# Forgetting attention with a gated convolution FFN: three half batches loaded plainly, decay rows by DMA, a rewritten order

## The chip, the core and the metric

The kernel runs on one core of a Trainium2 chip. The metric is device time in microseconds (us). The profile names the engines so: PE is TensorE (matmuls), PEld its weight loads, DVE is VectorE, ACT is ScalarE, POOL is GpSimd, and SP is SyncE, which here only issues DMAs. "ACTq" and "SPq" are rows of the queues of ACT and SP, in which DMAs are issued. L12 means line 12 of the kernel; as the change adds lines, the same code has other line numbers after it.

## The reference, cut to what matters

```python
scores = scale * np.matmul(q, k.transpose(0, 1, 3, 2))        # (8, 8, 576, 576), scale = 1/8
cum    = np.cumsum(np.log(np.clip(f, 0.0001, 1.0)), axis=-1)
decay  = cum[:, :, :, None] - cum[:, :, None, :]
scores = np.where(causal, -1000000000.0, scores + decay)
attn   = softmax(scores)
x      = np.matmul(attn, v)          # 8 batches, 8 heads, 576 tokens, 64 per head -> (8, 576, 512)
h      = np.maximum(x @ w_in, 0.0)   # (8, 576, 1024)
conv   = sum of three taps over the tokens, each channel with its own weights
out    = (h * sigmoid(conv)) @ w_out # (8, 576, 512)
```

## The kernel before, in words

The 8 batches with 8 heads each are taken as 16 **half batches** hb of four heads; two neighbouring heads make a pair p. For each half batch q and k lie with the head's 64 dimensions on the partitions and the 576 tokens along the row, in tiles named `qk` (four in a ring, so half batch 4 takes the tile of half batch 0). A score block is a product of 128 columns of k with up to 512 columns of q, over all 128 rows: q and k come as float32 whose 16 upper bits are used as bfloat16, so odd rows hold the data and even rows would hold the lower halves. The even rows are overwritten: in a few of them stand the **decay rows** (the cumulated log gates, in two bfloat16 parts, against rows of one and minus one), so that one product gives score and decay together; the others are zero.

How q and k come in differs by half batch:

- Half batches 0 and 1 (`NPL = 2`) are loaded plainly into tiles `hg` (`load_plain`, tasks `ld`), turned by nine PE transposes of 128x128 for each pair and side (`turn_qk`, L165, tasks `tp`), and written into `qk` by ACT (L171) or DVE (L173) in one operation of 128 rows which also replaces the even rows by constants (`turned_qk`, tasks `cl`).
- Half batches 2 to 15 come by a transposing DMA from SP (L179, tasks `q`), and for 2 to 7 DVE then replaces the even rows (`clamp`, L185).
- The decay rows: the gates f are loaded twice, on 128 rows; DVE clips them (L519, task `dca`), ACT takes the logarithm (L265, `dcl`), DVE sums them up (L269, `dcs`) and writes the tile `kc` (L272, L273, `dck`). Three DMAs on SP write `kc` into a tensor `image` in DRAM (L278, `ki`), and for each half batch from 1 on two small DMAs bring its rows back into `qk` (L201 and L202, task `rw`). Half batch 0 does not wait for that (`PAIRS = 2`): each of its score products is followed by two more products, with `sel_k` and `kc` (L314) and with `kc` and `sel_q` (L316), which add the decay.

Per half batch, the score tasks are `st` (the last 64 tokens of the four heads), `sd` (diagonal blocks of a pair) and `so` (the blocks off the diagonal, one task for each head). Half batches 0 to 7 get their causal mask by a product with `mask` ahead of the diagonal blocks (L319), the others by POOL. ACT takes the exponentials: `et` (L331), `ed` (L352), `eo` (L369). Then follow the product with v (`pv`, L388 and L393; v is loaded in five pieces by `v` and cast to 16 bits by `va` on POOL, ACT or DVE), the normalization on DVE (`n` L402, `m` L404), and the turning of x (`t` L413 on PE with `tx` L416 on DVE, or one DMA).

When both half batches of a batch b are turned, its FFN runs over eight column blocks ff: product (`f`, L428), relu on ACT (`r`, L438), two convolution steps on DVE (`c` L444, `d` L446), tanh or sigmoid on ACT (`a`, L449), gate on DVE (`g`, L456, L454). When the eight gates are done, the second product (`o`, L463 and L467) runs in five chunks, each copied out by ACT or DVE (`e`, L473, L478) and stored (`s`).

**What sets the order.** The program text is one long list, `ORDER`, of some 1,070 task names; `Plan.play` emits the tasks in that order, so that each engine's queue is the list cut to its own tasks, run strictly one after the other. A name behind `@` is the engine or queue chosen for the task. Buffers are given out in the order of the list too. PE's results go through only four PSUM tiles, `ps` 0 to 3: a task that wants one waits until the reader of an earlier task has emptied it. An engine that waits for one task holds all that stands behind it in its queue.

## Time and profile before

| | |
|---|---|
| device time, three runs | 250.19, 250.32 and 251.66 us; median 250.32 |
| the profiled execution | span 249.0 us from the first to the last instruction; the page gives it no device time of its own, so the median of the runs stands 1.3 us above its span |
| PE, DVE, ACT, POOL busy | 230.2, 210.3, 206.7, 54.3 us |
| TensorE clock that the throttle granted | 1.000 of full speed over the whole span |
| DMA | 49.70 MB, mean 200 GB/s |

The busy time of PE says only that a matmul was under way, and short matmuls overlap; so the length of a task on PE is read from start to start, not from the durations of its matmuls. Rows of the timeline merge instructions of one line that follow each other ("x36"). A number in brackets, or behind the bar, is the idle time just before, and the arrow names what ended it. Rows of stretches give each engine's busy time between two moments.

### The profile page before, as it was taken

The numbers are of one execution on the slowest core, as the hardware profiler recorded it, in microseconds if no ns is written. First come the engines' busy times: TensorE is split into PE (matmuls) and PEld (weight loads), VectorE is DVE, ScalarE is ACT, GpSimd is POOL, SyncE is SP. The second block draws the span as 40 slices with busy tenths as digits, with TensorE's granted clock in tenths as the row PEclk, the third lists the DMA queues.
The fourth block names the chain that finished last, engine by engine and source line by source line (L and its number), as shares of the span: only waits on it lengthen the run. The fifth ranks groups of instructions, "written<-read, shape, count | busy, mean of one in ns | idle before, by whom it ended". The sixth has DMA issues, their size and how long they took to land.

```text
span 249.0 us, 6606 instructions
## 1 busy us (share of the span) xinstructions
PE 230.2 (92%) x2723; PEld 148.7 (60%) x2723; DVE 210.3 (84%) x326; ACT 206.7 (83%) x280; POOL 54.3 (22%) x76
## 2 busy tenths in 40 slices
PE   0898989769999999999999999999999999999992
PEld 0786675447755675666566756576675557454440
DVE  5727077999999999989999979999989899999840
ACT  2754985999998999998998899998999997678632
POOL 8001500051300040045005352229240420000000
PEclk9999999999999999999999999999999999999999
DMA  7979999999999999999999999899999930705055
GB/s 188 303 165 235 270 211 209 220 175 279 256 186 222 196 176 276 239 234 197 196 305 240 227 204 200 203 232 202 216 178 303 176 106 22 163 0 192 0 191 190
DMA packets 120849, 49.70 MB, mean 200 GB/s; under 512 B 109919, under 2 KB 111455, under 8 KB 120819
## 3 DMA queue, kind: packets, MB, share of 16 engines
q1 hardware_dynamic: 120573, 48.91, 92.0%
q8 instruction: 21, 0.34, 0.6%
q10 hardware_dynamic: 246, 0.37, 0.6%
q14 instruction: 9, 0.07, 0.1%
HBM read 21.11 MB, written 10.17 MB: 126 GB/s over the span
## 4 chain that ended last, share of the span: by engine, by line
PE 69%; DVE 9%; ACT 8%; DMA 6%; SPq 4%; issue 2%; ACTq 0%; DVEq 0%
PE ps L428 20%; PE ps L463 19%; PE ps L311 12%; PE ps L388 5%; DVE u L446 3%; ACT pp L369 3%; SPq L179 3%; PE ps L467 2%; DMA qk<-in_q_dram 2%; DVE hg L456 2%; DMA pd<-in_moe_conv_w_dram 2%; ACT pp L352 2%; DVE u L444 2%; DMA vf<-in_v_dram 2%; PE ps L165 2%
## 5 line engine op out<-in xcount | busy, mean ns | idle before, releaser
L428 PE MATMUL ps<-xt,w_in_f 128*128 128x512 f16 (+1 forms) x512 | 68.8, 286 | 1.8 <-ACT pp L369 1.3
L369 ACT ACTIVATE pp<-ps 128x1024 f16<-128x1024 f32 x64 | 64.6, 1034 | 2.7 <-PE ps L311 1.4
L311 PE MATMUL ps<-qk 128*128 128x128 bf16 (+2 forms) x576 | 63.0, 241 | 1.5 <-ACT pp L352 0.5
L463 PE MATMUL ps<-w_out_f,hg 128*128 128x512 f16 x256 | 58.9, 379 | 0.0
L446 DVE SCALAR_TENSOR_TENSOR u<-ht,cwt,u 128x576 f32<-128x576 f16 x64 | 55.7, 886 | 0.7
L444 DVE SCALAR_TENSOR_TENSOR u<-ht,cwt 128x576 f32<-128x576 f16 x64 | 52.8, 838 | 2.3 <-ACT ht L438 2.0
L449 ACT ACTIVATE hg<-u,cw 128x576 f16<-128x576 f32 x64 | 48.4, 782 | 4.8 <-DVE u L446 4.6
L428 PEld LDWEIGHTS <-w_in_f 128*128 128x128 f16 x512 | 33.7, 98 | 31.2 <-issue 2.7
L311 PEld LDWEIGHTS <-qk 128*128 128x128 bf16 x576 | 39.1, 98 | 20.4 <-issue 3.5
L438 ACT ACTIVATE ht<-ps 128x576 f16<-128x576 f32 x64 | 41.4, 657 | 7.2 <-PE ps L428 4.8
L456 DVE SCALAR_TENSOR_TENSOR hg<-hg,ht 128x576 f16<-128x576 f16 x51 | 41.9, 837 | 0.5 <-ACT hg L449 0.5
L463 PEld LDWEIGHTS <-hg 128*128 128x128 f16 x256 | 23.8, 98 | 25.8 <-issue 0.2
L355 POOL TENSOR_SCALAR_AFFINE_SELECT pp<-pd 128x1024 f16<-128x1024 f32 x16 | 21.1, 1330 | 60.2 <-ACT pd L352 60.1
L388 PE MATMUL ps<-va,pp 128*128 128x65 f16 x640 | 24.5, 193 | 0.3 <-ACT pp L352 0.2
L216 POOL CAST va<-vf 128x1024 f16<-128x1024 f32 x11 | 14.2, 1315 | 46.3 <-DMA qk<-image 20.6
L404 DVE TENSOR_TENSOR xm<-ps,rc 128x896 f16<-128x896 f32 (+1 forms) x32 | 23.8, 751 | 0.4
L388 PEld LDWEIGHTS <-pp 128*128 128x128 f16 x640 | 22.6, 97 | 2.5 <-issue 0.4
L352 ACT ACTIVATE pp<-ps 128x1024 f16<-128x1024 f32 x16 | 16.4, 1037 | 2.4 <-PE ps L316 1.6
L352 ACT ACTIVATE pd<-ps 128x1024 f32<-128x1024 f32 x16 | 16.2, 1027 | 1.4 <-PE ps L311 1.1
L473 ACT COPY ob<-ps 128x1024 f32<-128x1024 f32 (+1 forms) x17 | 13.2, 785 | 4.8 <-PE ps L467 1.8
L319 PE MATMUL ps<-mask,ident 128*128 128x512 bf16 (+1 forms) x40 | 14.5, 363 | 2.8 <-ACT pp L369 1.3
L185 DVE TENSOR_SCALAR qk<-qk,lim 128x2304 uint16<-128x2304 uint16 x12 | 10.1, 865 | 1.3 <-DMA qk<-in_q_dram 1.3
(87 smaller groups left out, 184.2 us busy)
## 6 DMA issues: line engine op xcount, KB each, us to landing
...
```

The costliest lines, as they stand in the source:

```text
L311: nc.tensor.matmul(o, tk[:, h * S + k0:h * S + k0 + 128], tq[:, h * S + q0:h * S + q0 + n], start=first, stop=last and not by_matmul(hb, h))
L352: nc.scalar.activation(o, ps_of(f"sd{i}").rearrange("p (s c) -> p s c", s=2), AF.Exp, scale=SCALE)
L369: nc.scalar.activation(pair(i)[:, s, 512:1536], ps_of(f"so{i}.{s}"), AF.Exp, scale=SCALE)
L388: nc.tensor.matmul(ps[:, c:c + D + 1], block(hb, h, m, n), va[:, h, m, 0:D + 1], start=(m == 0), stop=(m == n))
L404: nc.vector.tensor_tensor(xm[:, CUT * D * u:CUT * D * u + nj * k * D].rearrange("p (j x d) -> p j x d", x=k, d=D), got[:, :, :, 0:D], r.un ...
L428: nc.tensor.matmul(ps[:, t0:t1], w_in_f16[:, cc, 128 * ff:128 * (ff + 1)], xt[:, cc // 2, x:x + t1 - t0], start=(cc == 0), stop=(cc == NCC ...
L438: nc.scalar.activation(ht_of(b, ff)[:, 2:2 + S], ps_of(f"f{b}.{ff}")[:, 0:S], AF.Relu, scale=1.0 if (b, ff) in LATE else 0.5)
L444: nc.vector.scalar_tensor_tensor(u, ht[:, 1:1 + S], cwt[:, ff, 0:1], ht[:, 2:2 + S], op0=ALU.mult, op1=ALU.add)
L446: nc.vector.scalar_tensor_tensor(u, ht[:, 3:3 + S], cwt[:, ff, 1:2], u, op0=ALU.mult, op1=ALU.add)
L449: nc.scalar.activation(hg_of(b, ff), u_t[slot[f"c{b}.{ff}", "u"]], AF.Sigmoid if (b, ff) in LATE else AF.Tanh, scale=cw[:, ff, 1:2])
L456: nc.vector.scalar_tensor_tensor(hv, hv, 1.0, ht_of(b, ff)[:, 2:2 + S], op0=ALU.add, op1=ALU.mult)
L463: nc.tensor.matmul(ps[:, 512 * (c % 2):512 * (c % 2 + 1)], hg_of(b, ff)[:, 128 * c:128 * (c + 1)], w_out_f16[:, ff, :], **kw)
```

## The change

It is done in these parts:

1. `NPL = 3`: half batch 2 too is loaded plainly; its two transposing DMAs and two clamps go.
2. Only the upper 16-bit halves are turned: five PE transposes for each pair and side (L166 after), of 128 columns, and of 64 for the last. Two copies (L173 after) put them into rows 0 to 63 of `qk`. The decay rows of half batches 0 to 2 stand in rows 64 to 66 beside rows of one and minus one, which POOL sets by `memset` (`unit_rows`); score products of these half batches run over 67 rows.
3. `PAIRS = 0`: half batch 0 gets its decay rows by DMA like the others, and the 72 products with `sel_k` and `sel_q` go. `ki` is now issued by ACT in two DMAs; `rw0` and `rw2` are issued by ACT, `rw1` by POOL.
4. The gates are loaded once, on 64 rows; `kc`'s second half is computed from them.
5. Constants are split: some stay ahead of everything, others become tasks (`k1`, `k2` on DVE, `k3` and `kr2` on POOL). The load of the exp table becomes a task (`xp`).
6. Eight products of zeros (`warm_up`, four tasks `wu`) stand first on PE; the transposes of the convolution weights (`cw`), which stood first, come later.
7. `ORDER` is another list altogether, for the whole program. Of 16 large casts of v 12 are on POOL instead of 11, of the small ones 8 instead of 6.

PE where the first scores begin, before (`qk_85` is the tile of half batch 0, `hg_125` the plain load):

```order
L165 LDWEIGHTS hg_125
L165 MATMUL ps_131<-ident_b,hg_125 128x128
L319 LDWEIGHTS ident
L319 MATMUL ps_132<-mask,ident 128x512
L311 LDWEIGHTS qk_85
L311 MATMUL ps_132<-qk_85 128x128
L314 LDWEIGHTS kc
L314 MATMUL ps_132<-sel_k,kc 128x128
L316 LDWEIGHTS sel_q
L316 MATMUL ps_132<-kc,sel_q 128x128
```

The same place after:

```order
L166 LDWEIGHTS hg_125
L166 MATMUL ps_131<-ident_b,hg_125 64x128
L338 LDWEIGHTS ident
L338 MATMUL ps_132<-mask,ident 128x512
L330 LDWEIGHTS qk_85
L330 MATMUL ps_132<-qk_85 128x128
```

The two extra products behind each score product are gone; and ahead of this place now stand the transposes of both half batches 0 and 1 (eight sets of five), where before only the four sets of half batch 0 did and those of half batch 1 stood behind the first scores.

ACT's queue at the start, before:

```order
L265 ACTIVATE u_121<-u_121 128x576
L266 ACT_TABLE_LOAD
L171 ACTIVATE qk_85<-ps_131,lim 128x1152
L171 ACTIVATE qk_85<-ps_132,lim 128x1152
L171 ACTIVATE qk_85<-ps_133,lim 128x1152
L352 ACTIVATE pp_95<-ps_132 128x2x512
```

And after, from the logarithm (L284) to the first exponential (L371); `image` is the tensor in DRAM, `qk_86` the tile of half batch 1:

```order
L284 ACTIVATE u_121<-u_121 64x576
L544 ACT_TABLE_LOAD
L295 DMA image<-kc 64x576
L296 DMA image<-kc 128x576
L173 COPY qk_85<-ps_132 64x128x5
L173 COPY qk_85<-ps_132 64x128x4
L206 DMA qk_85<-image 1x2304
L207 DMA qk_85<-image 2x2304
L173 COPY qk_86<-ps_131 64x128x5
L173 COPY qk_86<-ps_131 64x128x4
```

Behind these rows come two more copies, from the same `ps_131` into `qk_85`, and then the first exponential. Four DMAs stand in this queue now, two of which read what the first two wrote; and the copies that empty `ps_131` stand behind them.

POOL, after, behind its constants (`qk_87` is the tile of half batch 2); before, the casts stood directly behind the constants:

```order
L264 MEMSET qk_87 3x2304
L265 MEMSET qk_87 1x2304
L206 DMA qk_86<-image 1x16x144
L207 DMA qk_86<-image 2x2304
L221 CAST va_91<-vf_89 128x4x4x64
```

The same pair of memsets for `qk_85` and `qk_86` now opens POOL's queue, in place of three memsets (L252 to L254) that became the later task `k3`.

The diff, cut to its core (the two lists are shown by their first words):

```diff
 ORDER = """
-dca cw ld0 ld1 ld0.0.0 tp0.0.0 dcl ld0.1.0 ld0.0.1 tp0.0.1 tp0.1.0 v0.0 ld0.1.1 ld1.0.1 ld1.0.0 dcs dck q2.1 ki@SP
...
+wu0 wu1 wu2 wu3 ld0 ld0.0.0 kr2 dca ld1 k2 dcl xp ld1.0.1 ld1.0.0 tp1.0.0 dcs dck ki@ACT ld0.1.0 ld0.0.1 tp1.0.1
...
-    NPL = 2
-    PAIRS = 2
+    NPL = 3
+    PAIRS = 0
...
     def turn_qk(hb, p, side):
         o = ps_of(f"tp{hb}.{p}.{side}").bitcast(BF16)
-        i = raw(hb)[:, 2 * side + p, :].bitcast(BF16)
-        for j in range(9):
-            nc.tensor.transpose(o[:, 128 * j:128 * (j + 1)], i[:, 128 * j:128 * (j + 1)], ident_b)
+        i = raw(hb)[:, 2 * side + p, :].bitcast(BF16).rearrange("r (x w) -> r x w", w=2)
+        for x in range(5):
+            n = min(128, 9 * D - 128 * x)
+            nc.tensor.transpose(o[0:n, 128 * x:128 * (x + 1)], i[:, 128 * x:128 * x + n, 1], ident_b)
 
     def turned_qk(hb, p, side, e):
-        t = (stq_t, stk_t)[side][hb % RING].bitcast(U16)[:, 2 * p * S:2 * (p + 1) * S].rearrange("r (t j) -> r t j", j=9)
...
+        t = (stq_t, stk_t)[side][hb % RING][0:D, 2 * p * S:2 * (p + 1) * S].rearrange("r (t j) -> r t j", j=9)
+        o = ps_of(f"tp{hb}.{p}.{side}").bitcast(BF16)
+        for y in range(2):
+            i = o[D * y:D * (y + 1), 0:128 * (5 - y)].rearrange("r (j t) -> r t j", t=128)
+            (nc.scalar.copy if e == "ACT" else nc.vector.tensor_copy)(t[:, :, y:9:2], i)
...
-    def rows_of(hb):
+    def rows_of(hb, e="SP"):
         h0 = 2 * PAIRS if hb == 0 else 0
         c = slice(hb * HH + h0, (hb + 1) * HH)
...
+        if hb < NPL:
+            rq, rk = stq_t[hb % RING][D:D + 1, h0 * S:HS], stk_t[hb % RING][D + 1:D + 3, h0 * S:HS]
+        else:
+            rq, rk = even_rows(hb, 0, 1, 0, HS), even_rows(hb, 1, 2, HS, 2 * HS)
+        QUEUE[e].dma_start(rq, image[0, 0:1, c, :].rearrange("j h s -> j (h s)"))
+        QUEUE[e].dma_start(rk, image[1, 1:3, c, :].rearrange("j h s -> j (h s)"))
...
-    nc.scalar.dma_start(fsb[BH:128], f.rearrange("b h s -> (b h) s"))
...
+    def unit_rows(hb):
+        nc.gpsimd.memset(stq_t[hb][D:D + 3, :], 1.0)
+        nc.gpsimd.memset(stk_t[hb][D:D + 1, 0:HS], -1.0)
+
+    for hb in range(0 if PAIRS < 2 else 1, 2):
+        unit_rows(hb)
...
     def decay_image(e):
-        for j, a, h in ((0, 0, 0), (1, 1, 0), (2, 1, 1)):
-            {"SP": nc.sync, "POOL": nc.gpsimd}[e].dma_start(image[j, a], kc[BH * h:BH * (h + 1)])
+        QUEUE[e].dma_start(image[0, 0], kc[0:BH])
+        QUEUE[e].dma_start(image[1, 1:3].rearrange("j h s -> (j h) s"), kc)
...
     def scores(o, hb, h, k0, q0, n, m=128, first=True, last=True):
-        tq, tk = stq_t[hb % RING], stk_t[hb % RING]
+        rows = 128 if hb >= NPL else D if by_matmul(hb, h) else D + 3
+        tq, tk = stq_t[hb % RING][0:rows], stk_t[hb % RING][0:rows]
...
-    for x in range(0):
-        add(f"wu{x}", "PE", [], lambda x=x: warm_up(f"wu{x}"), take=["ps"])
+    for x in range(4):
+        add(f"wu{x}", "PE", [], lambda x=x: warm_up(f"wu{x}"), take=["ps"], give=[("ps", f"wu{x}")], behind=[f"wu{x - 1}"] if x else [])
...
-    add("ki", "SP", ["dck"], lambda: decay_image("SP"))
+    add("ki", "SP/ACT/POOL", ["dck"], decay_image)
...
-                add(f"rw{hb}", "SP", [f"cl{hb}.{p}.{side}" for p, side in parts] + ["ki"], lambda hb=hb: rows_of(hb))
-                ready = [[f"rw{hb}"]] * 2
+                add(f"rw{hb}", "SP/ACT/POOL", ["ki"] + ([f"kr{hb}"] if hb > 1 else []), lambda e, hb=hb: rows_of(hb, e))
+                ready = [[f"cl{hb}.{p}.{side}" for side in range(2)] + [f"rw{hb}"] for p in range(2)]
```

108 lines of the change are left out of this document (55 added, 53 removed).

## The prediction

> **What bounds the kernel now.** I read the stretches first, then PE's waits, then the timeline of the start. The rows of stretches give, behind the length, the busy time of each engine.
>
> ```profile
> span 249.0 us, 6606 instructions
> 7.09:12.03 4.94, 4.93 (x45) 4.75 (x45) 3.92 (x11) 4.53 (x5) 0.00 (x0) 1.00 1.20 332
> 12.03:26.51 14.48, 13.36 (x150) 10.39 (x149) 6.42 (x9) 8.37 (x9) 1.04 (x1) 1.00 0.89 192
> 26.51:38.22 11.71, 10.86 (x205) 8.65 (x204) 5.47 (x11) 10.26 (x12) 3.07 (x3) 1.00 1.21 235
> 38.22:60.00 21.78, 18.28 (x212) 11.51 (x210) 20.10 (x27) 19.02 (x27) 4.56 (x4) 1.00 1.06 218
> 60.00:120.00 60.00, 59.59 (x751) 39.01 (x752) 57.85 (x87) 56.31 (x77) 12.57 (x13) 1.00 1.09 225
> 120.00:180.00 60.00, 59.47 (x752) 38.44 (x752) 56.31 (x80) 56.11 (x78) 20.71 (x19) 1.00 1.11 221
> 180.00:210.00 30.00, 29.48 (x399) 19.15 (x394) 28.28 (x44) 29.09 (x42) 7.01 (x6) 1.00 0.78 164
> 210.00:244.20 34.20, 34.20 (x228) 16.75 (x226) 28.59 (x45) 21.32 (x33) 0.00 (x0) 1.00 0.38 110
> 244.20:249.00 4.80, 0.01 (x2) 0.00 (x0) 0.00 (x0) 0.42 (x2) 0.00 (x0) 1.00 0.58 191
> PE ps L293 <- DMA pd<-in_moe_conv_w_dram: 7.1, 1, 7.1
> ```
>
> From 60 us to its last matmul at 244.2 PE idles 1.5 of 184 us: that part is bound by PE's work and cannot get shorter unless work goes. PE's other idle time lies in three places: 7.1 us ahead of its first instruction, 3.5 us between 38.22 and 60, and 4.8 us at the end. So the change can only gain in the first 60 us. The moment that hands over from start to steady state is the first FFN product:
>
> ```profile
> 38.22 4.08 PE L428 MATMUL ps<-xt,w_in_f 128*128 128x512 f16 x32
> ```
>
> I call it f0.0. Behind it lie 249.0 - 38.22 = 210.8 us. Behind its f0.0 the changed kernel has nearly the same work: one transfer of the ledger is that before, `sd4`, `so4.0` and `sd5` were already done there, while after, `sd6`, `so6.1` and `so6.0` are. So the sum is: f0.0 after, plus 210.8, plus that difference, plus or minus what the new list does to the idle time behind it.
>
> **The price of a score task.** From start to start, with products and without:
>
> ```profile
> 20.13 0.38 PE L319 MATMUL ps<-mask,ident 128*128 128x512 bf16 x1 [0.54 <-ACT qk L171]
> 21.90 0.19 PE L311 MATMUL ps<-qk 128*128 128x64 bf16 x1
> 23.21 0.27 PE L319 MATMUL ps<-mask,ident 128*128 128x256 bf16 x1
> 26.51 0.38 PE L319 MATMUL ps<-mask,ident 128*128 128x512 bf16 x1
> 27.39 0.38 PE L319 MATMUL ps<-mask,ident 128*128 128x512 bf16 x1
> 96.40 0.44 PE ps L311 x4
> ```
>
> `sd1` with products takes 21.90 - 20.13 = 1.77, a plain `sd3` 27.39 - 26.51 = 0.88; an `so` with products 23.21 - 21.90 = 1.31, a plain one 0.44. The ledger difference is (2 x 0.88 + 0.44) - (0.88 + 2 x 0.44) = +0.4 us. Without products, half batch 0 costs PE 2 x 0.9 + 4 x 0.87, some 5.3 us less (more in `st0`); but this is no gain by itself, since ACT sets the pace there: a half batch has six large exponentials.
>
> ```profile
> 57.96 1.83 ACT pp L369 x2
> 14.73 1.02 ACT L352 ACTIVATE pp<-ps 128x1024 f16<-128x1024 f32 x1 [1.55 <-PE ps L316]
> 34.09 1.02 ACT L352 ACTIVATE pp<-ps 128x1024 f16<-128x1024 f32 x1
> ```
>
> One costs 0.915 us. Those of half batches 0 and 1 run from 14.73 to 34.09 before (the row at 34.09 is half batch 2's): 19.4 us for twelve of them, 11.0 us of work, since copies by L171 and waits for the slow score products lie between. After, the copies stand ahead of all exponentials and PE no longer holds them up. What is lost is the early beginning at 14.73, since the decay rows now go through DRAM.
>
> **The new beginning, step by step.**
>
> ```profile
> 6.97 0.46 DVE L519 TENSOR_SCALAR u<-u 128x576 f32<-128x576 f32 x1 [2.70 <-DMA u<-in_f_dram]
> 0.81 0.55 ACTq L221 DMA_DIRECT2D u<-in_f_dram  x1
> 2.06 4.89 DMA pd<-in_moe_conv_w_dram
> 10.07 0.76 DVE L273 SCALAR_TENSOR_TENSOR kc<-u,kc 64x576 bf16<-64x576 f32 x1
> L278 SPq DMA_DIRECT2D image<-kc x3: 525/545/584, 13.0 to 14.2; - x3
> 24.52 0.71 SPq L202 DMA_DIRECT2D qk<-image  x1
> PEld L311 <- DMA qk<-image: 0.9, 1, 0.9
> L237 DVE TENSOR_TENSOR lit<-lit 128x1 f32<-128x1 f32 x1 | 0.2, 159 | 0.0
> ```
>
> *Gates.* The clip began at 6.97, when the second gate load had come; the third transfer of that queue took 4.9 us from issue. A single load issued at 0.81 lands between 2.9 (2.1 us, the least of these rows, below) and 6.97; I take 4.9 from its issue, 5.7. From clip to the end of `kc` it was 10.83 - 6.97 = 3.9 us; `k2` (some ten operations like L237, 0.16 us each, most of them beside the logarithm) adds 0.5: `kc` at 10.1.
>
> *Image.* Two issues of 0.545 on ACT: 11.2. No row shows when such a write lands. Bounds: 2.1 us from issue (`rw1`, issued at 24.52, had landed when its first product ran at 26.6, after a wait of 0.9) and the 4.9 of the conv weights, issued among the same early loads. I take 2.8, near the first, and 14.0.
>
> *ACT's queue.* `rw0` waits for that, and all of ACT behind it. Its issues cost what L201 and L202 do on SP, 0.27 + 0.58: 14.9. Then comes the copy that empties `ps_131`, 1.3 us:
>
> ```profile
> L171 ACT ACTIVATE qk<-ps,lim 128x1152 uint16<-128x1152 uint16 x5 | 6.2, 1310 | 0.0
> 8.07 3.95 PE ps L165 x36
> 13.57 0.11 PE ps L311
> 13.75 0.06 PE ps L316
> ```
>
> (the new pair of copies moves the same 1152 columns; at worst it costs 0.2 more, at best half). At 16.2 `tp0.1.1` may run, five transposes of 0.11: `sd0` at 16.8. The rows of `rw0`, 14.9 + 1.4, are there before it.
>
> *Clock.* The trace shows matmuls at half pace until 13.6: 0.11 us for 128 columns against 0.06 after. The zero products end by some 4.7 us (eight of 512 columns at four times 0.11), and then PE waits for loads, and again from about 13 to 16. Bounds for `sd0`, `so0.0`, `so0.1`: 1.76 us if warm, 3.5 if cold; I take cold, as PE was after its idle 7.1 us: they end at 20.3.
>
> [...]
>
> *POOL.* `sd2` needs `rw1`, which stands on POOL behind its memsets and those of `qk_87`:
>
> ```profile
> 2.28 1.05 POOL L254 MEMSET zero<- 64x1152 bf16 x1
> 1.16 0.57 POOL L252 MEMSET pd<- 64x576 bf16 x1
> 6.17 0.31 POOL L262 MEMSET va<- 64x256 f16 x1
> ```
>
> By columns, 2304 take 2.1 us (1.05 x 2). Four from 1.16 end at 9.6; the other constants took from 3.3 to 6.48, 3.2: 12.8; two more: 17.0. Two DMA issues, at SP's 0.85 or twice that, and 1.4 us to land: 19.3 to 20.1, just ahead of 20.3. Fewer partitions could make the memsets cheaper; then nothing changes. Here 1 us more on POOL is 1 us more at the end.
>
> *Exponentials.* `ed0` at 18.5, `eo0.1` and `eo0.0` until 22.1; `sd2`, `so2.0`, `st1` are ready by 21.9. Then nine large ones and two small (0.28): 22.1 + 9 x 0.915 + 0.56 = 30.9, where before it was 34.09. From there to f0.0 before: 38.22 - 34.09 = 4.1 us of `pv1`, the norm and the turn. I keep it: **f0.0 at 35.0, 3.2 us earlier.**
>
> **Behind f0.0.** PE waited there for exponentials (1.3 us, the longest):
>
> ```profile
> PE ps L428 <- ACT pp L369: 1.3, 1, 1.3
> 43.16 0.78 ACT L449 ACTIVATE hg<-u,cw 128x576 f16<-128x576 f32 x1 [1.15 <-DVE u L446]
> 100.89 0.99 PE ps L388 x32
> ```
>
> ACT itself stood waiting for DVE with exponentials behind. Up to the next batch's first FFN product the new list holds two more `sd`, three more `so` and the two halves of one more `pv` (0.99 for 32 products, some 0.87 for 28), 4.9 us more for PE, but only four more large exponentials less one tanh of 0.78, 2.9 for ACT. So 2.0 of the 3.5 us of idle time are filled; bounds 0 and 3.5. Of the other edits: clamps and DMA transposes of half batch 2 (on no row that PE waits for) make room for twelve pairs of copies instead of eight copies; the casts of v moved to POOL, which is idle most of the time, cost nothing while its casts end ahead of `pv`. The end is alike: five chunks, PE full to the last matmul, one copy, one store.
>
> Sum: 249.0 - 3.2 + 0.4 - 2.0 = 244.2, and 1.3 from span to the median of the runs: 245.5. Each wait on this way can only be later than planned, so I round up to **246.0 us**.
>
> **The rivals.**
>
> *The rows come late.* If the small transfers beside SP's loads take the 4.9 us of the conv weights, the image lands at 16.1, `rw0` is issued at 17.0 and lands at 21.9, so `sd0` starts there and not at 16.8: f0.0 at 40.1, and 249.0 + 1.9 + 0.4 - 2.0 + 1.3 = 250.6, no change. For it speaks the DMA share of 1.20 from 7 to 12 us; against it `rw1`'s 2.1 us at a share of 0.89. Chance 0.28.
>
> [...]
>
> *The new list is slower in the steady state.* It sets 15 of the 64 gates within two places behind their tanh, where before it was 4. DVE then waits for ACT, in order, with convolution steps behind.
>
> ```profile
> L449 ACT ACTIVATE hg<-u,cw 128x576 f16<-128x576 f32 x64 | 48.4, 782 | 4.8 <-DVE u L446 4.6
> ```
>
> Eleven more, each a full tanh of 0.78, are 8.6 us of DVE, which has 2.2 + 3.7 + 1.7 = 7.6 us to spare from 60 to 210. None covered: 246.0 + 8.6 = 254.6. It ends slower by over 1% once 6.8 of the 8.6 fall where PE waits. Against it: such waits cost DVE only 0.5 us here. For it: DVE at 96% leaves no place to make up. Chance 0.25.
>
> *Everything fits.* Image and rows in 2.1 us, warm clock, the idle time filled: f0.0 some 0.7 + 1.7 = 2.4 earlier and 1.5 less idle: 246.0 - 3.9 = 242.1. Chance 0.12.
>
> **How the numbers follow.** Forecast 0.35, late rows 0.28, slower list 0.25, all fits 0.12. A measurement of this kernel can tell about 1%: below 247.8 is faster, above 252.8 slower. That is 0.35 + 0.12 = 0.47, 0.28 and 0.25. The range leaves out half of the last case and most of the worst part of the slower one: 242.0 to 253.5.
>
> **What would show it.** First exponential near 18.5, first product L428 after near 35, its wait rows; the image's landing by when ACT issues `rw0` (14.0); POOL's DMA rows at 17.0; PE idle between f0.0 and 60 under 2 us, and from 60 on 1.5 us or less. I am wrong if ACT or POOL stands on its DMA past 20 us, or if DVE shows waits for L468 (the tanh after) of several us.

## The result: slower, and the profile after

| | before | after | forecast |
|---|---|---|---|
| device time, median | 250.99 us (250.19 to 252.13) | 270.5 us (269.06 to 272.95) | 246.0 us, range 242.0 to 253.5 |
| ratio, 95% interval | | 1.0805 (1.0729 to 1.0881) | 0.98 |
| span of the profiled execution | 249.0 us | 271.1 us | 244.2 us |
| f0.0, first FFN product | 38.22 us | 46.79 us | 35.0 us |
| behind f0.0 | 210.8 us | 224.3 us | 209.2 us |

The profiled execution of after took 272.95 us, the longest of its four; so the split below adds up to 22.1 us where the medians differ by 19.5. All ratios, here and below, leave out executions that took over 1.5% longer than the fastest of their kernel, and the profiles of b_qlate (271.84 us) and b_eng (280.46 us) are of such slow ones.

The split by f0.0, in the rows of stretches, for before (L428):

```profile
0.00:38.22 38.22, 29.16 (x396) 23.83 (x397) 19.17 (x48) 24.45 (x25) 9.49 (x35) 1.00 1.01 224
38.22:249.00 210.78, 201.02 (x2330) 124.86 (x2327) 191.12 (x279) 182.27 (x255) 44.85 (x41) 1.00 0.92 195
```

and for after (L447); the columns are length, busy time of PE, PEld, DVE, ACT and POOL, granted clock, DMA share, GB/s:

```profile
0.00:46.79 46.79, 35.27 (x314) 22.98 (x315) 29.57 (x55) 23.69 (x27) 23.55 (x44) 0.67 0.82 189
46.79:271.10 224.31, 205.18 (x2335) 126.23 (x2333) 202.62 (x282) 181.41 (x250) 52.73 (x45) 0.99 0.88 181
```

Two losses: 8.6 us ahead of f0.0, at a mean granted clock of 0.67, and 13.5 us behind it. Behind it DVE is busy for 11.5 us more, PE idles 19.1 us instead of 9.8, and POOL is busy for 7.9 us more.

**The start.** In after's timeline ACT issues the two DMAs of `rw0` and then makes its copies, and PE waits for them:

```profile
11.31 0.36 ACTq L296 DMA_DIRECT2D image<-kc  x1
15.63 0.25 ACTq L206 DMA_DIRECT2D qk<-image  x1
18.79 0.25 ACTq L207 DMA_DIRECT2D qk<-image  x1
20.79 0.83 PE L166 MATMUL ps<-ident_b,hg 128*128 128x128 bf16 x5 [3.63 <-ACT qk L173]
21.55 0.61 PE L338 MATMUL ps<-mask,ident 128*128 128x512 bf16 x1
23.93 1.02 ACT L371 ACTIVATE pp<-ps 128x1024 f16<-128x1024 f32 x1 [0.66 <-PE ps L330]
35.25 2.38 PE L407 MATMUL ps<-va,pp 128*128 128x65 f16 x40 [0.26 <-ACT pp L388]
40.89 1.42 PE L407 MATMUL ps<-va,pp 128*128 128x65 f16 x40
32.00:36.00 4.00, 3.74 (x31) 2.31 (x29) 0.00 (x0) 2.85 (x4) 1.36 (x2) 0.50 0.00 0
```

The second write of the image was issued at 11.31 and its reader could be issued only at 18.79. The first scores stand at 21.55; and from there PE is full at half pace (40 products take 2.38 us at 35.25 and 1.42 us at 40.89), while ACT stands waiting for it (0.66 us ahead of the first exponential, 1.32 ahead of one at 32.47). The image is not the only thing that is late here: DVE, with its copies and the constants, is busy for 9.60 of the 10 us from 10 to 20.

**Loads.** From 32 to 40 us the DMA engines move nothing (share 0.00, 0 GB/s). SP's queue and what came of it:

```profile
39.88 2.55 SPq L178 DMA_TRANSPOSE qk<-in_q_dram  x1
SPq L178 <- PE ps L330: 28.6, 5, 12.6
62.44 1.91 PE L407 MATMUL ps<-va,pp 128*128 128x65 f16 x40 [2.92 <-ACT va L223]
```

`q5.0`, the transfer at 39.88, needs the tile of half batch 1, whose scores were late; behind it stood the loads of v of batch 1, whose product then came late (the row at 62.44).

**The steady part.** PE's waits in after (us in total, times, longest):

```profile
PE ps L447 <- DVE ob L492: 3.9, 2, 2.7
PE ps L330 <- DVE xt L435: 1.7, 1, 1.7
PE ps L407 <- DVE xm L423: 1.7, 2, 1.2
```

DVE, which released PE for 1.7 us behind f0.0 before, is now the releaser of most of PE's waits, with 10.1 us in seven such rows. And its FFN operations are longer, though their work is the same:

```profile
L465 DVE SCALAR_TENSOR_TENSOR u<-ht,cwt,u 128x576 f32<-128x576 f16 x64 | 59.6, 950 | 0.6
L463 DVE SCALAR_TENSOR_TENSOR u<-ht,cwt 128x576 f32<-128x576 f16 x64 | 55.0, 867 | 2.7 <-ACT ht L457 2.6
L475 DVE SCALAR_TENSOR_TENSOR hg<-hg,ht 128x576 f16<-128x576 f16 x51 | 44.3, 882 | 1.4 <-ACT hg L468 1.4
```

Before it was 886, 838 and 837 ns. The median of one is unchanged (815 ns at L465, 814 before); a few take twice as long (over 1.4 us: 20 in these three lines, 10 before). Where, the timelines of POOL and DVE show, in after:

```profile
122.79 4.67 POOL L374 TENSOR_SCALAR_AFFINE_SELECT pp<-pd 128x1024 f16<-128x1024 f32 x3 [2.40 <-ACT pd L371]
122.55 0.81 DVE L465 SCALAR_TENSOR_TENSOR u<-ht,cwt,u 128x576 f32<-128x576 f16 x1
123.28 1.65 DVE L463 SCALAR_TENSOR_TENSOR u<-ht,cwt 128x576 f32<-128x576 f16 x1
124.86 3.21 DVE L465 SCALAR_TENSOR_TENSOR u<-ht,cwt,u 128x576 f32<-128x576 f16 x2
```

and in before, where the first of two such masks lies beside an operation of DVE that reads PSUM:

```profile
132.60 1.18 POOL L355 TENSOR_SCALAR_AFFINE_SELECT pp<-pd 128x1024 f16<-128x1024 f32 x1 [15.06 <-ACT pd L352]
133.73 1.71 POOL L355 TENSOR_SCALAR_AFFINE_SELECT pp<-pd 128x1024 f16<-128x1024 f32 x1
132.74 1.08 DVE L404 TENSOR_TENSOR xm<-ps,rc 128x896 f16<-128x896 f32 x1
133.74 0.75 DVE L456 SCALAR_TENSOR_TENSOR hg<-hg,ht 128x576 f16<-128x576 f16 x1
```

In after the FFN operations beside these masks take 1.65 us and, two of them, 3.21, where the one before them takes 0.81; and the three masks take 1.56 each, where the shortest of the 16 takes 1.10. In before the mask at 132.60 lies beside L404, which reads PSUM, and both are near what they take at other places (1.18, the shortest of the 16 being 1.09; 1.08, and 1.09 for L404 at 102.20 with no work on POOL beside it); the one at 133.73 starts with L456, an FFN operation, and takes 1.71, while L456 keeps its median of 0.75.

### The profile page after: what moved, and what is told of

Read it like the earlier page. It is cut to its first block, busy times and chain, and to the rows that moved or that the text cites. A ratio compares the mean times of both kernels' runs of the same rounds, so it can differ in the third digit from the quotient of the medians.

```text
span 271.1 us, 6478 instructions
## 1 busy us (share of the span) xinstructions
PE 240.4 (89%) x2647; PEld 149.2 (55%) x2647; DVE 232.2 (86%) x336; ACT 205.1 (76%) x277; POOL 76.3 (28%) x89
## 4 chain that ended last, share of the span: by engine, by line
PE 48%; DMA 19%; DVE 19%; ACT 4%; SPq 3%; issue 3%; POOL 2%; DVEq 0%; POOLq 0%
PE ps L447 13%; PE ps L482 12%; DMA vf<-in_v_dram 10%; PE ps L330 8%; PE ps L407 6%; DVE u L465 5%; DVE hg L475 5%; DMA qk<-in_q_dram 5%; DMA qk<-blank 4%; DVE u L463 3%; PE ps L338 3%; SPq L178 2%; PE ps L486 2%; PE ps L412 2%; POOL va L221 2%
## 5 line engine op out<-in xcount | busy, mean ns | idle before, releaser
L447 PE MATMUL ps<-xt,w_in_f 128*128 128x512 f16 (+1 forms) x512 | 70.8, 286 | 5.7 <-DVE ob L492 3.9
L330 PE MATMUL ps<-qk 128*128 128x64 bf16 (+5 forms) x576 | 63.9, 253 | 3.1 <-DVE xt L435 1.7
L465 DVE SCALAR_TENSOR_TENSOR u<-ht,cwt,u 128x576 f32<-128x576 f16 x64 | 59.6, 950 | 0.6
L463 DVE SCALAR_TENSOR_TENSOR u<-ht,cwt 128x576 f32<-128x576 f16 x64 | 55.0, 867 | 2.7 <-ACT ht L457 2.6
L330 PEld LDWEIGHTS <-qk 128*128 128x128 bf16 (+1 forms) x576 | 41.5, 103 | 23.5 <-issue 6.9
L447 PEld LDWEIGHTS <-w_in_f 128*128 128x128 f16 x512 | 33.9, 98 | 34.7 <-issue 6.7
L475 DVE SCALAR_TENSOR_TENSOR hg<-hg,ht 128x576 f16<-128x576 f16 x51 | 44.3, 882 | 1.4 <-ACT hg L468 1.4
L374 POOL TENSOR_SCALAR_AFFINE_SELECT pp<-pd 128x1024 f16<-128x1024 f32 x16 | 23.8, 1498 | 45.6 <-ACT pd L371 45.6
L371 ACT ACTIVATE pp<-ps 128x1024 f16<-128x1024 f32 x16 | 16.5, 1033 | 6.8 <-PE ps L330 6.8
L421 DVE RECIPROCAL rc<-ps 128x14 f32<-128x14 f32 (+1 forms) x32 | 6.7, 208 | 16.2 <-PE ps L407 13.2
L371 ACT ACTIVATE pd<-ps 128x1024 f32<-128x1024 f32 x16 | 16.3, 1024 | 2.6 <-PE ps L330 2.3
L166 PE MATMUL ps<-ident_b,hg 128*128 128x128 bf16 (+1 forms) x60 | 8.5, 275 | 9.6 <-ACT qk L173 3.6
L338 PE MATMUL ps<-mask,ident 128*128 128x512 bf16 (+1 forms) x40 | 16.9, 425 | 0.0
```

What stands on the lines that cost most here:

```text
L330: nc.tensor.matmul(o, tk[:, h * S + k0:h * S + k0 + 128], tq[:, h * S + q0:h * S + q0 + n], start=first, stop=last and not by_matmul(hb, h))
L338: nc.tensor.matmul(o, ident, mask[:, 0:j].unsqueeze(1).broadcast_to((128, n, j)), start=True, stop=False)
L371: nc.scalar.activation(o, ps_of(f"sd{i}").rearrange("p (s c) -> p s c", s=2), AF.Exp, scale=SCALE)
L447: nc.tensor.matmul(ps[:, t0:t1], w_in_f16[:, cc, 128 * ff:128 * (ff + 1)], xt[:, cc // 2, x:x + t1 - t0], start=(cc == 0), stop=(cc == NCC ...
L463: nc.vector.scalar_tensor_tensor(u, ht[:, 1:1 + S], cwt[:, ff, 0:1], ht[:, 2:2 + S], op0=ALU.mult, op1=ALU.add)
L465: nc.vector.scalar_tensor_tensor(u, ht[:, 3:3 + S], cwt[:, ff, 1:2], u, op0=ALU.mult, op1=ALU.add)
```

## The experiments

Times are medians; each is compared with before as run on the same chip (250.99 to 251.79 us). "f0.0" and "behind" are of the profiled execution.

| kernel | time | ratio to before | f0.0 | behind |
|---|---|---|---|---|
| after | 270.5 | 1.0805 (1.0729 to 1.0881) | 46.8 | 224.3 |
| a_rows128 | 268.55 | 1.0686 (1.0659 to 1.0714) | 43.3 | 223.5 |
| a_nowu | 271.62 | 1.0767 | 42.8 | 227.2 |
| a_kisp | 270.74 | 1.0777 | 47.7 | 222.1 |
| a_pairs2 | 286.33 | 1.136 | 63.2 | 222.0 |
| b_qlate | 271.27 (266.22 to 272.99) | too scattered for one | 46.3 | 222.9 |
| b_eng | 278.08 | 1.0942 (1.0843 to 1.1042) | 56.5 | 221.4 |
| b_qeng | 268.37 | 1.0693 (1.0621 to 1.0764) | 44.0 | 221.2 |
| c_pool12 | 256.45 | 1.0203 (1.0127 to 1.0278) | 37.8 | 218.7 |
| h_tail | 265.63 | 1.0559 (1.0494 to 1.0625) | 52.5 | 211.5 |
| h_head | 270.81 | 1.0749 (1.0671 to 1.0828) | 50.9 | 217.7 |
| h_tailq128 | 259.81 | 1.0323 (1.0259 to 1.0387) | 48.3 | 210.2 |
| d_wu | 251.64 | 1.0019 (0.9981 to 1.0058) | 37.2 | 210.5 |
| x_after | 266.36 | 1.0601 (1.0529 to 1.0674) | 44.0 | 219.5 |
| x_before | 250.26 | 0.9967 (0.9932 to 1.0003) | 37.9 | 211.1 |
| p2_rows128 | 271.09 | 1.0805 (1.0733 to 1.0878) | 46.3 | 222.3 |
| h_all | 265.08 | 1.056 (1.0493 to 1.0626) | 52.8 | 212.0 |
| x_afterq128 | 258.33 | 1.0297 (1.0217 to 1.0377) | 43.8 | 213.5 |
| m_late | 272.29 | 1.0866 (1.076 to 1.0972) | 44.1 | 224.9 |

### Is it the start?

**a_rows128**

```diff
-        nc.gpsimd.memset(stq_t[hb][D:D + 3, :], 1.0)
-        nc.gpsimd.memset(stk_t[hb][D:D + 1, 0:HS], -1.0)
+        nc.gpsimd.memset(stq_t[hb][D:128, :], 1.0)
+        nc.gpsimd.memset(stk_t[hb][D:128, 0:HS], -1.0)
...
-        rows = 128 if hb >= NPL else D if by_matmul(hb, h) else D + 3
+        rows = 128
```

> Changed kernel, but the score products of half batches 0 to 2 run over all 128 rows instead of 67 (rows 67 to 127 hold ones in q and minus ones in k, which adds the same number to all scores of a row, and the softmax takes it out); the memsets have the same count and columns. Theory A: products over 67 rows do not raise TensorE's clock. Then the granted clock goes from 0.50 to 1.00 some 4 us after the first scores (21.5), near 25 to 26 instead of 39; the first FFN product comes near 41 instead of 46.8, and the time is 262 to 266 us instead of 270.5. Rival: the clock stays low for another reason (the idle times of PE, the load of the engines); then it rises near 39 as before and the time is 269 to 272.

The pace rose by 28.2 us instead of 39, the pair of `pv0` products cost what it should, and f0.0 came 3.5 us earlier. Two rows, the first its granted clock, the second the first `pv`:

```profile
28.00:32.00 4.00, 3.52 (x41) 2.51 (x40) 0.00 (x0) 3.58 (x6) 2.48 (x4) 1.00 0.65 200
32.84 1.59 PE L407 MATMUL ps<-va,pp 128*128 128x65 f16 x40 [0.32 <-ACT pp L388]
```

The exponentials of half batches 0 and 1 took 13.5 us (23.91 to 37.38), where after takes 17.3. But the time fell by 2.0 us only, and the part behind f0.0 stayed at 223.5 us.

**a_nowu**

```diff
-    for x in range(4):
+    for x in range(0):
         add(f"wu{x}", "PE", [], lambda x=x: warm_up(f"wu{x}"), ...
```

> Changed kernel without the eight zero products. Theory: the clock that they release is lost again at 8.6 us, before any work that needs it; the time stays within 0.5% of 270.5, and the first scores stay near 21.5. Rival: they help the first transposes; then the transposes of half batch 1 end 1 us or more later, and the time is 271.5 or more.

271.62 against 270.5 us: the zero products are worth nothing at the end. f0.0 came 4 us earlier, with the pace at full from about 30 us on, and what lies behind took 2.9 us longer.

**a_kisp**

```diff
-... xp ld1.0.1 ld1.0.0 tp1.0.0 dcs dck ki@ACT ld0.1.0 ld0.0.1 ... v0.0 v0.2 ... v0.4 ... ld0.1.1 v0.1
+... xp ld1.0.1 ld1.0.0 tp1.0.0 dcs dck ld0.1.0 ld0.0.1 ld0.1.1 ki@SP v0.0 v0.2 v0.4 ... v0.1
```

> Changed kernel with the image written from SP's queue and the loads of v and half batch 3 placed behind it in that queue. Theory: the image took 7.1 us from issue to landing because the loads of v were queued ahead on the same DMA engines; then it lands 2.5 to 4 us after issue, near 15, the first scores come near 18 instead of 21.5, the time is 266 to 268. Rival: a write to DRAM takes that long by itself; then it lands near 18.5 as before, and the time is 270 or more, since v comes later too.

On SP, ahead of the loads of v, the second write was there 1.9 us after its issue:

```profile
13.34 0.35 SPq L296 DMA_DIRECT2D image<-kc  x1
15.19 0.24 ACTq L207 DMA_DIRECT2D qk<-image  x1
```

So the writes were not slow by themselves. That it was the loads ahead of them fits, but the run also moves the writes to another queue and does not tell the two apart. The chain still ended only 1.7 us earlier (first exponential at 22.26), since PE now waited 3.6 us for a load of q, and the time did not move.

**a_pairs2**

```diff
-    PAIRS = 0
+    PAIRS = 2
```

(and `rw0` left out of the list)

> Changed kernel with the decay of half batch 0 by products again (72 products over 128 rows more, 64-row score products, no rw0 on ACT, one pair of memsets less on POOL). Theory: the first scores wait for ACT, which stands on the image until 19.1, and the clock needs products of 128 rows. Then the first scores come near 17.5 instead of 21.5, the clock is at 1.00 by 22 to 23, the first FFN product near 40, the time 259 to 264. Rival: DVE, which POOL's memsets hold up, sets the first scores; then they stay at 20 or later and the time is 267 or more.

16 us slower than after, far above the 259 to 264 us of the theory; the rival's "267 or more" holds, but not for its reason alone. Half batch 0 goes by products again, as before, but here its score products run over 64 rows, and PE stayed at half pace until past 41 us. See p2_rows128 below. The run also shows what the image cost: without `rw0` in ACT's queue the first scores stood at 19.66, only 1.9 us earlier than in after, and were released there by a copy on DVE. For the first scores that is the rival.

None of the four moved the end as far as it moved f0.0, and what lies behind stayed at 222 to 227 us in all of them. That spoke for a second cause.

### The loads, the engines, and POOL by itself

**b_qlate**

```diff
-... rw2@ACT wi3 q5.0 v1.0 q5.1 t0 wi2 v1.1 wic3@POOL wic2@POOL q4.1 ... v1.2 ... v1.3 ... v1.4
+... rw2@ACT wi3 v1.0 wi2 v1.1 v1.2 v1.3 v1.4 q5.0 q5.1 q4.1 t0 wic3@POOL wic2@POOL
```

> After with another order on SP alone: v1.0 to v1.4 and wi2 stand ahead of q5.0, q5.1 and q4.1, so that no load waits behind a transfer whose ring slot is still in use. Theory Q (the loss behind f0.0 comes from the pause of the loads between 32 and 41 us and the late v behind it): the pause goes, PE's idle time at 58.5 to 62.4 us goes, POOL's wait for v falls from 28.7 us to under 16, and the time is 262 to 266. Theory D (behind f0.0 VectorE is the bound: it was busy for 202.6 of 224.3 us there, against 191.1 of 210.8 before, so that the idle time is the same): the pause goes, but VectorE still has 201 to 204 us of work behind f0.0, and the time is 268 to 271.

PE's wait for v at 62 us went, as theory Q has it, but POOL's waits for v grew (55.6 us, off the path). One execution took 266.22 us, just above theory Q's range; the other three took 270.69 to 272.99, in or above theory D's. So this run does not decide between them; that the late v is the main cause it does not show.

**b_eng**

```diff
-wic0@DVE ... va0.1@POOL ... wic3@POOL wic2@POOL ... va3.1@POOL va2.1@ACT ... va5.0@POOL ... va7.0@DVE ...
+wic0@POOL ... va0.1@DVE ... wic3@ACT wic2@DVE ... va3.1@DVE va2.1@POOL ... va5.0@ACT ... va7.0@POOL ...
```

(19 tasks in all)

> After, with the engine of each cast of v, of the weights and of each copy of xt set as in the kernel before (7 casts leave GpSimd, 5 of VectorE's and GpSimd's go to ScalarE in sum); order and loads are those of after. Theory D: the three long VectorE operations of the FFN come back from 950, 867 and 882 ns to within 20 ns of 886, 838 and 837, VectorE's work behind f0.0 falls from 202.6 to 194 to 198 us, and the time to 262 to 266. Theory Q: no change, 269 to 272.

Slower in all four executions (274.29 to 280.46 us). The cast of `wi2` now stands on DVE, and `wi2` waits on SP behind `q5.0`:

```profile
DVE w_in_f L530 <- DMA ob<-in_moe_w_in_dram: 7.9, 1, 7.9
```

In the profiled execution f0.0 slid to 56.5. On POOL that wait had cost PE 0.4 us at most (L447 for `w_in_f`, after). The engines cannot be judged with SP's order as it is.

**b_qeng** (both edits)

> Both edits: v1 and wi2 ahead of q5 and q4.1 on SP, and the engines of the kernel before for the casts. Theory D alone: 262 to 266 as with the engines alone; theory Q alone: 262 to 266 as with the order alone; both at work: 256 to 261, since the start (f0.0 at 46.8 against 38.2 us) stays as it is and 8.6 us over the kernel before are left.

268.37 us: SP's order frees the casts, but 221.2 us behind f0.0 are far from 211. Both theories missed; the list itself was left.

**c_pool12** (the kernel before)

```diff
+    for x in range(12):
+        add(f"xc{x}", "POOL", [], lambda: nc.gpsimd.tensor_copy(spare_o, spare_i))
```

(one behind every third or fourth POOL task of the list; `spare_i` is 128x1024 float32)

> The kernel before with twelve more GpSimd casts of 128x1024 from float32 to float16, of a tile that is never read, spread over the time from 50 to 200 us; all else as before. Theory D with a shared way to SBUF: each cast of about 1.25 us stretches the VectorE operation beside it by some 0.8 us, so VectorE's work behind f0.0 grows from 191 to 198 to 201 us, its FFN operations to 860 to 950 ns, and the time by 5 to 9 us to 255 to 260. Rival (GpSimd's work lies beside the rest and costs nothing, GpSimd being busy for a fifth of the span): within 1 us of before.

5.5 us slower, in the range of theory D; the interval of the ratio, 1.3 to 2.8%, lies clear of zero. Twelve casts that nobody reads cost DVE 6.4 us and the part behind f0.0 7.9 (that the two share a way to SBUF, as the theory has it, this does not show):

```profile
37.80:256.50 218.70, 203.72 (x2330) 125.33 (x2327) 197.53 (x279) 183.03 (x255) 61.46 (x53) 0.99 0.87 188
```

### Start or list?

The list was cut at f0.0 and the halves exchanged.

**h_tail** (after's list up to f0.0, with seven tasks added that before has ahead of it; then the rest in the order and on the engines of before)

```diff
-... eo6.1 so6.0 cl2.1.1@DVE f0.0 f0.1 eo6.0 v1.3 cl2.1.0@DVE f0.2 r0.0 st2 r0.1 sd7 ...
+... eo6.1 so6.0 cl2.1.1@DVE cl2.1.0@DVE sd4 so4.0 ed4 eo4.0 q4.0 sd5 f0.0 ed5 r0.0 f0.1 r0.1 c0.0 ...
```

> After up to the first FFN product f0.0, then everything that is left in the order, and on the engines, of the kernel before. Theory L (the list from f0.0 on is the worse one: it loads VectorE for 10 us at a time and then lets it wait, so that TensorE is idle for 19.1 us behind f0.0 where it was 9.8 before): f0.0 stays at 46 to 48 us, the time behind it falls from 224 to 211 to 215 us, and the time is 259 to 263. Theory S (what is lost behind f0.0 comes from the late start and the late loads, whatever the list): 267 to 272.

**h_head** (before's list up to f0.0, with ten tasks added that after has ahead of it; then the rest in after's)

```diff
-... sd5 f0.0 cl3.1 ed5 cl3.0 r0.0 f0.1 r0.1 c0.0 f0.2 r0.2 d0.0 ...
+... sd5 cl3.0 cl3.1 rw3 q5.0 q5.1 sd6 ed6 so6.1 eo6.1 so6.0 f0.0 f0.1 eo6.0 v1.3 f0.2 r0.0 ...
```

> The kernel before up to f0.0, with its loads of half batch 2 by transfers that transpose, and then everything that is left in the order, and on the engines, of after. Theory L: f0.0 stays at about 38 us, the time behind it grows from 211 to 220 to 225 us, and the time is 258 to 264. Theory S: 249 to 253, since the start and its loads are those of before.

**h_tailq128** (h_tail with the edits of b_qlate and a_rows128)

> As the run with after's start and the list of before behind f0.0, and with v1 and wi2 ahead of q5 and q4.1 on SP and products over 128 rows in the half batches 0 to 2. Theory L: f0.0 at 42 to 44 us, 211 to 215 us behind it, time 254 to 259. Theory S: f0.0 at 42 to 44 us, but 219 to 223 us behind it, time 262 to 266.

With the list of before the part behind f0.0 takes 210 to 212 us behind every start (before, d_wu, h_tail, h_tailq128, h_all), with after's 221 to 227 us behind all of after's starts. But f0.0 does not cut these lists at the same work: in h_tail PE does `sd4`, `so4.0` and `sd5` from 48.64 to 52.53 us, ahead of f0.0, and after does them behind it. So 3.9 us of the shorter part behind f0.0, and of the later f0.0, are tasks that changed sides (in h_tailq128 and h_all as well). A cleaner mark is the first FFN product of batch 1, f1.0: ahead of it before, h_tail, h_tailq128 and h_all have the same tasks of scores, `pv` and FFN.

| kernel | f1.0 | behind f1.0 |
|---|---|---|
| before | 66.3 | 182.7 |
| h_tail | 81.2 | 182.8 |
| h_tailq128 | 75.8 | 182.7 |
| h_all | 80.4 | 184.4 |
| h_head | 83.1 | 185.5 |
| after | 82.8 | 188.3 |

The stretches behind f1.0 of before, h_tail, h_tailq128 and after:

```profile
66.30:249.00 182.70, 176.79 (x2018) 108.68 (x2015) 164.75 (x242) 157.27 (x222) 37.95 (x36) 1.00 0.90 189
81.20:264.00 182.80, 176.99 (x2018) 108.63 (x2016) 164.19 (x242) 157.12 (x222) 38.72 (x35) 1.00 0.88 188
75.80:258.50 182.70, 176.75 (x2018) 108.49 (x2015) 164.06 (x242) 157.12 (x222) 38.10 (x35) 0.99 0.88 187
82.80:271.10 188.30, 174.99 (x1936) 105.42 (x1930) 170.74 (x242) 151.64 (x212) 42.80 (x36) 1.00 0.84 179
```

Behind f1.0 the list of before costs the same after three of after's starts as after its own, but for 1.7 us in h_all; after's list costs 5.6 us more with after's start and 2.8 more with before's, though fewer matmuls are left there (1936 instead of 2018). That is theory L, for this part. But the times missed its ranges. In h_tail the pace also rose later still, past 43 us. It reaches f1.0 14.9 us later than before, with before's list from f0.0 on; in time it got back 4.9 of the 19.5 us. So the exchange does not clear the start. h_head, with before's start, is as slow as after: there f0.0 slid to 50.9, since the added loads no longer fit (PE waited 9.7 us for the rows of a half batch), so it shows that the list is bad for that start, not by how much. The start with before's list costs 13.8 us (h_tail), before's start with after's list 19.0 (h_head), both together 19.5; how the two share the time ahead of f1.0 these runs do not tell.

**d_wu** (the kernel before)

```diff
-    for x in range(0):
+    for x in range(12):
         add(f"wu{x}", "PE", [], lambda x=x: warm_up(f"wu{x}"), take=["ps"])
```

(and the twelve first in the list)

> The kernel before with 24 products of zeros (128 rows, 512 columns) ahead of TensorE's first work, nothing else. If the pace of the first scores in the kernel before (half until 13.6 us) comes from TensorE's idle time until 7.1 us, the scores run at full pace from the first, the first exp starts about 0.7 us earlier than 14.7 us, and the time falls by 0 to 0.8 us. Rival: the transposes between let the clock fall again, or the copies on ScalarE are the bound, and nothing changes.

The scores ran at full pace from the first (0.06 us from start to start from 11.94 on), f0.0 came at 37.2 instead of 38.2, and the time did not change that can be measured.

### What in the list? And what of the clock?

**x_after, x_before**

```diff
+        if e == "POOL" and hb >= 4:
+            return
...
-        o = pair(i)[:, :, 0:512] if i // 2 in MASK_PE else pd_t[slot[f"ed{i}", "pd"]]
-        nc.scalar.activation(o, ps_of(f"sd{i}").rearrange("p (s c) -> p s c", s=2), AF.Exp, scale=SCALE)
+        o = pair(i)[:, :, 0:512]
+        nc.scalar.activation(o, ps_of(f"sd{i}").rearrange("p (s c) -> p s c", s=2), AF.Exp, scale=SCALE if i // 2 in MASK_PE else 0.0)
...
-                add(f"md{i}", "POOL", [f"ed{i}"], lambda i=i: diag_mask(i), give=[("pd", f"ed{i}")])
+                add(f"md{i}", "POOL", [f"ed{i}"], lambda: None, give=[("pd", f"ed{i}")])
```

(and the same for `et` and `mt`)

> After without most of GpSimd's work behind f0.0: the masks of half batches 8 to 15 are left out (their exps are of zero times the score), and the casts of v that stand on GpSimd are left out from half batch 4 on; order and loads are the same. Theory P (GpSimd's work stretches VectorE's): the FFN operations of VectorE fall from 158.9 to 146 to 150 us, the time behind f0.0 from 224 to 213 to 217 us, the time to 259 to 263. Theory B (it is the balance of the list between TensorE, ScalarE and VectorE): the time stays at 266 to 270.

> The kernel before with the same left out as in the run of after without most of GpSimd's work. Theory P: the FFN operations fall from 150.4 to 146 to 149 us only, since GpSimd's work lies beside VectorE's reads of PSUM in that list, and the time by 0 to 3 us to 247 to 250; so the two lists come from 13.5 to 4 to 7 us of each other behind f0.0. Theory B: the same time here, but the two lists stay 12 to 14 us apart.

Behind f0.0, x_after and then x_before:

```profile
44.00:263.50 219.50, 205.18 (x2335) 126.70 (x2333) 186.31 (x282) 180.83 (x250) 7.62 (x7) 0.98 0.88 186
37.90:249.00 211.10, 201.04 (x2330) 124.71 (x2327) 182.25 (x279) 182.12 (x255) 6.83 (x5) 1.00 0.91 194
```

DVE is relieved of 16.3 us in after's list and of 8.9 in before's, where POOL also had 7.9 us less to do. The FFN operations fell to 142.9 and 140.6 us, below both ranges. Time behind f0.0: 4.8 us less in after's, nothing in before's, where PE was the bound anyway. PE's own waits for POOL were only 0.7 us in after, so the gain came by way of DVE. Neither theory has it whole: POOL's work is some 5 us of the 13.5, and 8.4 us between the lists were left. (That f0.0 came at 44.0 in x_after and not at 46.8 is not POOL's doing: the pace rose earlier there, by 33.60 us, when 40 products of `pv` took 1.58.)

**p2_rows128** (a_pairs2 and a_rows128; in half batch 0 zeros in rows 64 to 127)

> After with the decay terms of half batch 0 added by products (as in the run with two pairs by products, 286 us), but every product of the half batches 0 to 2 over 128 rows, the rows without a term filled with zeros. Theory R (products over 64 or 67 rows keep TensorE at half pace): the pace is full within 7 us of the first score, by 27 us where it was half until 60 us, f0.0 comes at 39 to 46 us instead of 63.2, time 262 to 268. Rival (the mix of three products for each score is slow by itself, or the late loads hold it): f0.0 at 55 us or later, time 275 to 286.

In a_pairs2 a mask product of 512 columns still took 0.63 us at 41.37; here the same score product of 448 columns falls from 0.56 to 0.35 within 1.8 us, about 4.5 us after the first mask product at 19.65:

```profile
23.20 0.56 PE L333 MATMUL ps<-qk 128*128 128x448 bf16 x1
25.00 0.35 PE L333 MATMUL ps<-qk 128*128 128x448 bf16 x1
```

f0.0 came 16.9 us earlier than in a_pairs2, though not all of that is the pace: a_pairs2 also pays for changing the rows (last section). That is theory R, for the pace. The time, 271.09, is that of after and missed the range. The first scores stand at 19.65 here and at 12.03 before (eight copies and the constants on DVE come first), and the list behind is after's; that these two hold what the pace won is argued, not shown.

**h_all** (p2_rows128, the edit of b_qlate, and the list of before from f0.0 on)

> All mends together: half batch 0 by products over 128 rows, the other early products over 128 rows, v1 and wi2 ahead of q5 and q4.1, and the order and engines of the kernel before from f0.0 on. With theories R and L: f0.0 at 39 to 44 us, 210 to 212 us behind it, time 251 to 257, level with the kernel before at best. If something else of the start costs time: 258 to 264.

212.0 us behind f0.0, as expected, but shorter by 3.9 only through the tasks that changed sides; f0.0 at 52.8. Its first scores stood at 22.06, released by a copy on DVE, 10 us later than before's. The time is above both ranges. No version beat the kernel before.

**x_afterq128** (x_after with the edits of b_qlate and a_rows128)

> The run of after without most of GpSimd's work (masks of half batches 8 to 15 and GpSimd's casts of v from half batch 4 on left out), and also with v1 and wi2 ahead of q5 and q4.1 on SP and products over 128 rows in the half batches 0 to 2. If the three named causes (half pace, pause of the loads, stretched VectorE) add up: f0.0 at 41 to 43.5 us, 214 to 217 us behind it, time 257 to 261, so that about half of the 20 us is accounted for and the rest is the start's late image and the balance of the list. If they overlap: 262 to 266, no better than without GpSimd's work alone.

```profile
43.80:257.30 213.50, 202.36 (x2335) 125.09 (x2333) 184.59 (x282) 180.46 (x250) 3.59 (x3) 1.00 0.84 183
```

The causes add up, and more: behind f0.0 it falls from 224.3 to 213.5 us, within 2.7 of before, and the time by 12.2 us. Alone, leaving out POOL's work took 4.8 us off this part, the order of the loads 1.4 (b_qlate) and 128 rows 0.8 (a_rows128), 7.0 in sum; together they take 10.8. No run has the loads and the rows mended with after's list and POOL's work left in.

**m_late**

```diff
-    for hb in range(0 if PAIRS < 2 else 1, 2):
-        unit_rows(hb)
...
         nc.gpsimd.memset(ht_t[t][:, S + 2:S + 3], 0.0)
+    for hb in range(0 if PAIRS < 2 else 1, 2):
+        unit_rows(hb)
```

> After with the memsets of the unit rows of half batches 0 and 1 behind GpSimd's small memsets instead of ahead of them. If a GpSimd memset holds up a VectorE operation that works in SBUF until it ends: the cast and the comparison at 1.3 to 5.4 us (2.12 and 2.00 us) fall to about 0.4 and 0.8 us, and the operations on the gates (clamp 0.70, scan 1.34, kc 0.63 and 0.75 us) stretch by up to 2 us each instead. Rival (those two are slow for a reason of their own, as their data type): they stay at 2 us. The time in both cases: 268 to 272.

DVE in after, with POOL's memsets, and then in m_late:

```profile
1.28 2.01 POOL L264 MEMSET qk<- 3x2304 bf16 x1
3.24 2.10 POOL L265 MEMSET qk<- 1x2304 bf16 x1
1.26 2.12 DVE L236 CAST hfx<-hix 128x128 f32<-128x128 int32 x1
3.41 2.00 DVE L237 TENSOR_SCALAR ident_b<-hfx,lit 128x128 bf16<-128x128 f32 x1
```

```profile
1.26 0.46 DVE L236 CAST hfx<-hix 128x128 f32<-128x128 int32 x1
1.76 0.33 DVE L237 TENSOR_SCALAR ident_b<-hfx,lit 128x128 bf16<-128x128 f32 x1
9.29 1.34 DVE L287 TENSOR_TENSOR_SCAN u<-one,u 64x576 f32<-64x576 f32 x1
10.66 2.06 DVE L290 TENSOR_SCALAR kc<-u 64x576 bf16<-64x576 f32 x1
10.40 2.01 POOL L265 MEMSET qk<- 1x2304 bf16 x1
```

The length goes with the memset: the two constants are short again, and `kc`'s first operation, 0.63 us in after, takes 2.06. The scan beside the memset ahead of it kept its 1.34.

## Why the prediction was wrong, step by step

- **Gates, `kc`.** Right within 1.2 us: the clip began at 5.01 (5.7 forecast), `kc` was done at 11.28 (10.1). From clip to `kc` it was 6.3 us and not the 4.4 forecast, which the early clip partly hides. The difference is two constants of `k2` (at 5.64 and 5.76 in after), which took 2.05 and 1.93 us beside a memset instead of 0.16 each.
- **Image.** Forecast 14.0 between bounds of 2.1 and 4.9 us from issue; the second write needed about 7. The bounds were rows of other DMAs; whether it was the loads ahead of it or its queue that made this one slower, a_kisp does not tell apart. The pair of copies behind it took 1.60 us on ACT, just above the step's worst of 1.5. ACT's queue stood behind the image, as the step has it, and `sd0` stood at 21.55, 4.8 us late. The rival of the late rows had it at 21.9 (it was the image and not the rows that was late); its f0.0 of 40.1 missed by the clock. That its price came out is in part luck: with no image ahead of the first scores (a_pairs2) they still stood at 19.66, behind DVE's copies. DVE's queue, full from 10 to 20 us, is a term that the sum put at nothing.
- **Clock.** The step that failed in the start. "Bounds for `sd0`, `so0.0`, `so0.1`" let the pace be full from the fourth score task on, as in before 1.6 us after its first score product. It stayed at half until about 39 us. The exponentials of half batches 0 and 1 then took 41.2 - 23.9 = 17.3 us and not 12.4. With 128 rows it rose 11 us earlier and they took 13.5 (a_rows128), so most of the 4.9 is the rows; that score products over 67 rows might keep the pace down has no place among the step's bounds. Without zero products the end was the same (a_nowu: 271.62 against 270.5 us), which fits the step: it took the first scores as cold in spite of them. In before the rise came 1.6 us after the first score product, behind 4.0 us of transposes over 128 rows too (8.00 to 12.02); that these had a part in it is the author's guess, and no run tests it.
- **POOL.** Right: memsets of 2.0 to 2.4 us, the DMA of `rw1` at 16.84 (17.0). What the step did not see is what they cost DVE: the cast beside the first of them took 2.12 us, and 0.46 where the memsets came later (m_late).
- **f0.0.** 46.8 for 35.0: 4.8 at `sd0`, 0.7 to the first exponential, 4.9 in the exponentials, 1.5 from there to f0.0.
- **Behind f0.0.** The step that failed most: "nearly the same work" and "210.8, plus that difference". 209.2 forecast, 224.3 measured. The exchange of the lists shows that behind f1.0 the list is the cause (182.7 to 184.4 us with before's list after four starts, 188.3 in after); between f0.0 and f1.0, where the rest lies, it does not tell start and list apart. Three terms were costed at nothing. The first is POOL's work ("cost nothing while its casts end ahead of `pv`"), some 5 us. The others are SP's queue past `q5.0`, which the step did not follow to the load of v behind it, and the half pace that came again when PE had waited for that (the granted clock reads 0.88 from 60 to 64 us and 0.69 to 68). With POOL's work gone, loads in time and 128 rows take another 6.0 us off this part (x_afterq128); with it they took 1.4 and 0.8, each alone. The last 2.7 us stay unexplained.
- **The idle time of 2.0 us** between f0.0 and 60 was filled, by the step's own sign: PE idled 1.1 us there and 3.5 before, in a stretch that was 8.6 us shorter. It was no gain, since from 60 us to its last matmul PE idled 13.8 us where the sign for a right forecast was 1.5 or less.
- **The rival of the slower list** named the right place and engine, and the wrong mechanism: gates close behind their tanh. DVE's waits for ACT before the gate are 1.4 us in the row of L475, against 0.5 before, and over all 64 gates, with the 13 of L473 (L454 before), 1.6 against 2.0. The prediction's 0.5 left these 13 out. What DVE lost was length, not waiting.

The reading that misled was "bound by PE's work": PE was full before, but DVE did 191.1 of 210.8 us at the same time. So x_before gains nothing from 8.9 us less on DVE, while c_pool12 pays 7.9 us for 6.4 more: the kernel stood just short of its second bound.

Shown are these three: GpSimd's work cost DVE and time (twelve casts more 6.4 us of DVE and 5.5 of the time in c_pool12, most of it left out 16.3 less of DVE and 4.8 less behind f0.0 in x_after); products over 128 rows brought the full pace earlier (by 28.2 us instead of 39 in a_rows128, 4.5 us after the first mask product in p2_rows128); and before's list kept its time behind f1.0 (182.8 us in h_tail and 182.7 in h_tailq128, 182.7 before). Only argued is the share of SP's pause by itself, since b_qlate ran with the pace at half until past 41 us. Why the pace, with 67 rows, rose at anything from 30 us (a_nowu) to past 43 (h_tail) stays open, and so does how start and list share the time between f0.0 and f1.0.
